# q and k of two batches loaded in 1 KB pieces, cast on chip and transposed by products with the identity

## The chip, the cores and the metric

The kernel runs on one core of a Trainium2 chip. The metric is device time in microseconds (us) of one execution, lower is better. The core has a matrix engine (PE, with its weight loads shown apart as PEld), a vector engine (DVE), a scalar engine (ACT), a general engine (POOL) and a synchronising engine (SP). PE writes only to PSUM, a memory of eight banks of 512 fp32 columns by 128 partitions, from which DVE or ACT must copy ("evacuate") results to SBUF. Transfers from and to DRAM (HBM) are DMAs: here they are issued from POOL's queue or from SP's queue and are carried by the same 16 DMA engines.

## The reference

Inputs are q, k, v of shape 8 x 8 x 576 x 64 (batch, head, position, head dimension) and three weights, all fp32. A sliding-window attention with a distance bias per head is followed, batch by batch, by a token-mixing layer:

```python
scores = scale * np.matmul(q, k.transpose(0, 1, 3, 2))
rel = pos[:, None] - pos[None, :]
mask = (rel >= 0) & (rel < window)                      # window = 128
scores = np.where(mask, scores + bias[None], -1000000000.0)   # bias = -slope[h] * |rel|
attn = softmax(scores)
x = (attn @ v) with the heads side by side              # 8 x 576 x 512
wq = x @ w_q;  wk = x @ w_k                             # 512 -> 64
W_tok = scale * np.einsum('bsd,btd->bst', wq, wk)
mixed = np.einsum('bst,btd->bsd', W_tok, x)
out = np.maximum(mixed, 0.0) @ w_out                    # 8 x 576 x 512, fp32
```

## The kernel before, in words

All products run in fp16 with fp32 sums in PSUM. The 576 positions of a batch are four blocks of 128 and a tail of 64; tails are handled for two batches at once. For every batch `b` the kernel does these steps, whose names are used below:

- **Loads.** Tiles `nat` hold a block of q or k (index `j` is 0 for q, 1 for k; `n` is the block): partition = position, columns = 8 heads of 64. Tiles `vt` hold blocks of v with a column of ones beside each head; `natt` and `vtl` hold the tails. For batches 1 to 7 POOL issues these loads, and the DMA itself turns fp32 into fp16 (L501, L508, L512, L516). For batch 0 alone, SP loads q and k as fp32 into tiles `natf` (function `lf`, L549), in runs of 64 values (256 B), and DVE or ACT casts them into `nat` (names `Cq0.n`, `Ck0.n`, at L365 and L367, the copy helper).
- **TQ, ETQ.** PE transposes `nat` (L361, in transpose mode, fp16 into PSUM; 16 small products a block) so that the head dimension lies on the partitions, and DVE or ACT evacuates into `qkT` (L371 and L373, two fp16 values moved as one fp32 on ACT). Batch 0 is done one block at a time, the others two at a time. TT and ETT do the same for the tails.
- **QK, EXP, MUL.** For each block `g` and half of the heads `u`, PE computes scores (QK), ACT applies the exponential (EXP, L674) and DVE multiplies with a table that holds the exponential of the bias and zero outside the window (MUL, L681). The result is `pt`. The tables `bias` and `biasl` are made at the start.
- **PV, X.** PE multiplies `pt` with v; the ones column gives the sum of the weights, and DVE divides (L723, L724) to give `x`.
- **XT, WQ, WK, G, MX, RM, OUT, EO, DO.** The mixing layer, reordered so that no 576 x 576 matrix is formed: x is transposed, multiplied with w_q and w_k, G is a 64 x 512 product of wk and x, MX multiplies wq with G, RM applies max(0, .) and writes fp16, OUT multiplies with w_out, EO copies to an fp32 tile `osb` (L365, L367) and DO stores it (L913, L916).

The order of the instructions on each engine is made by a planner inside the kernel (class `Order`). Each step has a list of the engines that may run it with a time for each, its dependencies, and a wish for its place (the table `WANT`, one number for each step). The planner repeatedly takes the engine that can start first, and among the steps that could start there within 0.11 us the one with the lowest number. Its result is a fixed order; on the chip the engines wait for each other through semaphores. While the planner's time is below 30 us, `keep_busy` (L392) puts products with the zero tile `fill` into PE's gaps, as many as the planner expects to fit; they write to the PSUM pair that the next step will use.

Three more things matter below. Each of the two DMA queues has eight semaphores, taken in turn, so an issue waits until the eighth transfer before it on that queue has landed. The outputs of batches 0, 1, 6 and 7 are stored by SP as soon as they are made; those of batches 2 to 5 (`LATE`) are kept in SBUF buffers (`HELD` = 18, shared with `natf`) and stored by POOL once all loads have been issued. POOL runs its set-up (identity, index and mask tables, clearing of padding) ahead of most loads. ACT's table of functions is loaded by its first instruction.

Of the kernel before, what the change touches and what calls it, by code (L numbers as in the profile page):

```python
# [33 lines left out]
STRIDE = 14  # L34
# [3 lines left out]
HELD = 18  # L38
LATE = (2, 3, 4, 5)
COLD = 8.0  # L40
# [4 lines left out]
    "ident": -516.89, "idh": -64.27, "iota": -947.82, "dist": -823.27, "zeros": -897.48,  # L45
# [153 lines left out]
}  # L199


# [802 lines left out]
```

## Time and profile before

| what | value |
|---|---|
| runs | 146.28, 146.66, 148.61 us, median 146.66 |
| profiled execution | 147.05 us, of which 145.3 us from its first to its last instruction (its span) |
| granted PE clock, mean over the span | 0.988 of full speed |
| busy in the span | PE 126.8, PEld 80.0, DVE 116.7, ACT 114.3, POOL 104.8 us |
| moved by DMA | 25.64 MB in 117447 packets, 113072 of them under 512 B |
| POOL's loads of q and k | 56, 128 KB each as written, median 6.4 us to landing |
| POOL's loads of v | 32, 128 KB each, median 6.6 us to landing |
| SP's loads of batch 0 | 8, 256 KB each, medians 4.5 (q) and 4.8 us (k) to landing |

Busy time is the union of an engine's instructions. Matmul ends are modelled, so PE's share is an upper bound for its use. "to landing" counts from the issue to the last byte's semaphore. Rows of the timeline name the line, the engine, the operation and the tiles, output first, then how many instructions were merged, and in brackets the idle time before them with what ended it.

### The profile page before, as it was taken

To read this page: it belongs to the slowest core of one execution; us is meant where nothing else is said; L and a number is where in the kernel's file an instruction comes from. 1 tells how busy PE (TensorE), PEld (TensorE's weight loads), DVE (VectorE), ACT (ScalarE), POOL (GpSimd) and SP (SyncE) were. 2 spreads that over 40 slices of the span, in tenths; PEclk is the share of its full clock that TensorE was granted. 3 is DMA by queue.
4 is the path that set the end of the run, shared out by engine and by line. 5 is a ranking of instruction groups with operands and counts; after the bars stand their busy time and mean duration, and the time that the engine had idled before them with its cause. 6 is when DMAs were issued, how large, how long until landed. Compare 5 with 4: busy or idle time off the path is not lost.

```text
span 145.3 us, 5428 instructions
## 1 busy us (share of the span) xinstructions
PE 126.8 (87%) x2315; PEld 80.0 (55%) x2315; DVE 116.7 (80%) x256; ACT 114.3 (79%) x169; POOL 104.8 (72%) x139
## 2 busy tenths in 40 slices
PE   6858858888997899779998997989999999999990
PEld 2224546645774458645674575647767657566340
DVE  6977997599839698959979999799999999991410
ACT  3727895599588976899599986999889989956751
POOL 5999678999986997578999999998977701230000
PEclk9986999999999999999999999999999999999999
DMA  4999999999999999999999999999999941155255
GB/s 103 262 182 180 159 154 144 149 173 154 190 251 186 157 183 218 247 179 155 156 155 156 157 154 157 154 154 151 146 213 399 363 171 72 77 144 207 83 162 202
DMA packets 117447, 25.64 MB, mean 177 GB/s; under 512 B 113072, under 2 KB 114096, under 8 KB 117424
## 3 DMA queue, kind: packets, MB, share of 16 engines
q0 software_dynamic: 106336, 18.49, 155.3%
q1 hardware_dynamic: 11088, 6.82, 16.6%
q8 instruction: 18, 0.29, 0.8%
q14 instruction: 5, 0.04, 0.1%
HBM read 29.62 MB, written 9.44 MB: 269 GB/s over the span
## 4 chain that ended last, share of the span: by engine, by line
PE 48%; DVE 16%; ACT 16%; POOL 7%; DMA 6%; issue 4%; POOLq 0%; DVEq 0%; ACTq 0%
PE pair L358 41%; ACT pt L674 10%; PE pair L361 7%; DMA vt<-in_v_dram 6%; DVE pt L681 3%; DVE x L724 3%; POOL nat L501 2%; DVE rm L837 2%; ACT qkT L371 2%; DVE xT L373 2%; DVE qkT L373 1%; POOL vt L516 1%; DVE inv L723 1%; POOL natt L508 1%; DVE xtl L724 1%
## 5 line engine op out<-in xcount | busy, mean ns | idle before, releaser
L674 ACT ACTIVATE pt<-pair 128x1024 f16<-128x1024 f32 x64 | 62.8, 1038 | 6.1 <-PE pair L358 5.8
L681 DVE TENSOR_TENSOR pt<-pt,bias 128x1024 f16<-128x1024 f16 x48 | 31.7, 683 | 3.3 <-ACT pt L674 3.1
L516 POOL DMA_DIRECT2D vt<-in_v_dram x32 | 29.7, 949 | 3.7 <-DMA nat<-in_k_dram 1.9
L358 PE MATMUL pair<-wout_sb,rm 128*128 128x512 f16 (+1 forms) x132 | 31.5, 373 | 0.7 <-ACT pt L674 0.5
L501 POOL DMA_DIRECT2D nat<-in_q_dram x28 | 25.9, 931 | 3.3 <-DMA vt<-in_v_dram 1.1
L501 POOL DMA_DIRECT2D nat<-in_k_dram x28 | 25.7, 925 | 1.6 <-DMA vt<-in_v_dram 0.5
L358 PE MATMUL pair<-qkT 64*128 64x256 f16 (+2 forms) x320 | 22.8, 254 | 4.0 <-ACT qkT L371 2.6
L358 PE MATMUL pair<-vt,pt 128*128 128x65 f16 x512 | 22.6, 193 | 1.4 <-DMA vt<-in_v_dram 1.0
L358 PEld LDWEIGHTS <-pt 128*128 128x128 f16 x576 | 20.0, 97 | 5.8 <-issue 2.5
L724 DVE TENSOR_TENSOR x<-pair,inv 128x512 f16<-128x512 f32 x32 | 22.1, 691 | 1.1
L365 ACT COPY osb<-pair 128x512 f32<-128x512 f32 (+1 forms) x25 | 14.8, 590 | 6.9 <-PE pair L358 6.7
L371 ACT COPY qkT<-pair 128x1024 f32<-128x1024 f32 (+2 forms) x19 | 16.0, 842 | 4.5 <-PE pair L361 3.5
L358 PEld LDWEIGHTS <-qkT 64*128 64x128 f16 x320 | 11.2, 95 | 12.4 <-issue 5.9
L358 PEld LDWEIGHTS <-rm 128*128 128x128 f16 x132 | 11.4, 97 | 12.0 <-issue 1.1
L913 POOL DMA_DIRECT2D out_dram<-osb x16 | 8.8, 558 | 11.0 <-DVE osb L367 5.4
L361 PEld LDWEIGHTS <-nat 64*128 64x128 f16 x512 | 9.4, 96 | 6.8 <-issue 4.6
L361 PE MATMUL pair<-identh,nat 64*128 64x64 f16 x512 | 11.2, 192 | 1.8 <-DVE x L724 0.4
L358 PE MATMUL pair<-fill 128*128 128x512 f16 x23 | 9.0, 531 | 3.1 <-DVE qkT L373 1.2
L358 PE MATMUL pair<-xT,wqq_sb 128*128 128x256 f16 (+1 forms) x64 | 10.3, 287 | 0.8 <-DVE xT L373 0.8
L681 DVE TENSOR_TENSOR pt<-pt,biasl 128x1024 f16<-128x1024 f16 x16 | 10.8, 683 | 0.2 <-ACT pt L674 0.2
L837 DVE TENSOR_SCALAR rm<-pair 128x512 f16<-128x512 f32 x16 | 10.5, 681 | 0.1
L367 DVE COPY osb<-pair 128x512 f32<-128x512 f32 (+1 forms) x12 | 8.0, 665 | 2.8 <-PE pair L358 2.7
(65 smaller groups left out, 162.7 us busy)
## 6 DMA issues: line engine op xcount, KB each, us to landing
vt<-in_v_dram POOLq DMA_DIRECT2D x32, 128.0 KB, 6.6
out_dram<-osb POOLq DMA_DIRECT2D x16, 256.0 KB, 4.6
out_dram<-osb SPq DMA_DIRECT2D x15, 256.0 KB, 5.4
nat<-in_k_dram POOLq DMA_DIRECT2D x28, 128.0 KB, 6.4
nat<-in_q_dram POOLq DMA_DIRECT2D x28, 128.0 KB, 6.4
natf<-in_q_dram SPq DMA_DIRECT2D x4, 256.0 KB, 4.5
natf<-in_k_dram SPq DMA_DIRECT2D x4, 256.0 KB, 4.8
out_dram<-osb SPq DMA_DIRECT2D x6, 128.0 KB, 2.4
```

Source lines behind the costliest of these rows:

```text
L358: hold(nc.tensor.matmul(*a, **k))
L361: hold(nc.tensor.transpose(*a))
L365: hold(nc.scalar.copy(out_ap, in_ap))
L367: hold(nc.vector.tensor_copy(out=out_ap, in_=in_ap))
L371: hold(nc.scalar.copy(out_ap.bitcast(FP32), in_ap.bitcast(FP32)))
L501: return lambda: nc.gpsimd.dma_start(out=nat_s[b % NNAT][j][n], in_=src[b, :, P * n:P * n + P, :].transpose([1, 0, 2]))
L516: return lambda: nc.gpsimd.dma_start(out=vt_s[b % NV][t][:, :, 0:D], in_=v[b, :, P * t:P * t + P, :].transpose([1, 0, 2]))
L674: nc.scalar.activation(out=pt[:, 0:1024], in_=two(s.bank).rearrange("p e c -> p (e c)"), func=AF.Exp, scale=SCALE)
L681: ENG2[o.eng].tensor_tensor(out=pt[:, 0:1024], in0=pt[:, 0:1024], in1=bt, op=ALU.mult)
L724: nc.vector.tensor_tensor(out=x[r].rearrange("p (g h d) -> p g h d", g=2, h=4), in0=pxv[r, :, :, 0:64], in1=inv[r].unsqueeze(3).broadcast_ ...
L837: hold(nc.vector.tensor_scalar(out=out_ap, in0=in_ap, scalar1=0.0, scalar2=WSCALE, op0=ALU.max, op1=ALU.mult))
L913: q.dma_start(out=out[b, P * st:P * st + P, c], in_=osb)
```

## The change

Batches 0 and 1 (`WIDE` = 2) now both take the way over `natf`. A tile is loaded by two DMAs, one for the even and one for the odd heads; on each partition lie four consecutive positions of one head, 1 KB in one piece. The cast regroups the blocks of 64 so that a pair of heads lies side by side. In place of 16 transposes a block, 16 ordinary products with a 64 x 64 identity write fp32 into every 4th column of two PSUM banks, so that the four positions come out interleaved in the right order. Each bank holds the heads of one unit `u` and is evacuated by itself; the scores of a unit need only its own halves. All loads from POOL wait for a tiny copy (`gate`) that reads the second q tile. Batch 1's outputs join the late ones, `HELD` is 23 and serves all full-width outputs, `keep_busy` puts in more fills, and all of `WANT` is different, so that the order of nearly every engine changes. By the instruction order, ACT's first instruction is now a cast, and the load of its function table stands behind that cast's wait for the second DMA; the load of `wq` moves from POOL's first to its twelfth; PE has 56 products with `fill` where it had 23.

```diff
-STRIDE = 14
+STRIDE = 14.6
-HELD = 18
-LATE = (2, 3, 4, 5)
-COLD = 8.0
+HELD = 23
+LATE = (1, 2, 3, 4, 5)
+COLD = 6.0
+GATE = (0, 1)
+WIDE = 2
...
-        n = int((gap + 0.3) / (0.43 if op.start < COLD else 0.216)) if gap > 0.1 else 0
+        n = int((gap + 0.5) / (0.43 if op.start < COLD else 0.216)) if gap > 0.1 else 0
...
-        issue = add(*name, want, {"POOL": (occ, occ + 1.5)}, deps, lambda o: emit())
+        issue = add(*name, want, {"POOL": (occ, occ + 1.5)}, [*deps, *gate], lambda o: emit())
...
         def lf(j, n):
             natf = spool.tile([P, DM], FP32, name="natf", tag="late", bufs=HELD)
-            src = (q, k)[j][0, :, P * n:P * n + P, :].transpose([1, 0, 2])
+            src = (q, k)[j][b, :, P * n:P * n + P, :].rearrange("(c e) (g r) d -> e c g (r d)", e=2, r=4)
 
             def em(o):
-                nc.sync.dma_start(out=natf.rearrange("p (h d) -> p h d", h=H), in_=src)
+                for e in range(2):
+                    nc.sync.dma_start(out=natf[:, 256 * e:256 * e + 256], in_=src[e])
 
             def cv(o):
-                cp(o.eng, nat_s[0][j][n].rearrange("p h d -> p (h d)"), natf)
-
-            d = add("L" + "qk"[j], 0, f"f{n}", next(i), {"SP": (0.92, 1.55)}, [], em)
-            d = od.add("Q", 0, n, 0.0, {"Q": (0.92, 1.7)}, [d], lambda o: None)
-            loads[0, j, n] = add("C" + "qk"[j], 0, n, next(i), EV(0.62, 0.43), [d], cv)
+                cp(o.eng, nat_s[b][j][n].rearrange("p (r e) d -> p e r d", e=2),
+                   natf.rearrange("p (e r d) -> p e r d", e=2, r=4))
+
+            d = add("L" + "qk"[j], b, f"f{n}", next(i), {"SP": (0.68, 1.3)}, first[-1:], em)
+            first.append(d)
+            d = od.add("Q", b, n, 0.0, {"Q": (0.66, 1.2)}, [d], lambda o: None)
+            if (b, j, n) == (0, *GATE):
+                gate.append(add("gate", "", "", -50, {"POOL": (0.1, 0.12)}, [d],
+                                lambda o: nc.gpsimd.tensor_copy(out=seen, in_=natf[:, 0:1])))
+            loads[b, j, n] = add("C" + "qk"[j], b, n, next(i), EV(0.62, 0.43), [d], cv)
...
+    def add_tq0(b, n, want):
+        def quad(o, h):
+            return one((o.bank[0], h)).rearrange("p (j c t) -> p j c t", j=2, c=2)
+
+        def em(o):
+            for j in range(2):
+                for i in range(4):
+                    for h in range(2):
+                        r = slice(64 * h, 64 * h + 64)
+                        mm(quad(o, h)[:, j].rearrange("p c (g i) -> p i c g", i=4)[:, i],
+                           nat_s[b][j][n][r, 2 * i:2 * i + 2, :].rearrange("p a b -> p (a b)"), identh[r, r],
+                           start=True, stop=True)
+
+        t = add("TQ", b, n, want, pe(0.47), [loads[b, 0, n], loads[b, 1, n], idh], em, banks=2, mode=1)
+        tq[b, n] = t
+        evt[b, n] = []
+        for h in range(2):
+            def ev(o, h=h):
+                cp(o.eng, qkT_s[b][:, :, 2 * h:2 * h + 2, P * n:P * n + P], quad(t, h))
+
+            evt[b, n].append(add("ETQ", b, f"{n}.{h}", want + 0.6, EV(0.60, 0.69), [t], ev, frees=[t], half=h))
...
-            evt[b, n] = ev
+            evt[b, n] = [ev, ev]
...
-        need = [evt[b, g], evt[b, g + 1]] if g < 3 else [evt[b, 3], ett[b]]
+        need = [evt[b, g][u], evt[b, g + 1][u] if g < 3 else ett[b]]
...
-            held = b in LATE
-            box["o"] = spool.tile([P, n], FP32, name=f"osb{n}", tag="late" if held else f"osb{n}",
-                                  bufs=HELD if held else 5 if n == DM else 2)
+            box["o"] = spool.tile([P, n], FP32, name=f"osb{n}", tag="late" if n == DM else f"osb{n}",
+                                  bufs=HELD if n == DM else 2)
...
-        for ns in ([0], [1], [2], [3]) if b == 0 else ([0, 1], [2, 3]):
+        for n in range(4) if b < WIDE else ():
+            add_tq0(b, n, base(b, 0) - 4 + 1.5 * n)
+        for ns in ([0, 1], [2, 3]) if b >= WIDE else ():
```

More of the change, by code (lines that the diff above doesn't have):

```diff
@@ L37 @@
 LAG = 0.5
-HELD = 18
-LATE = (2, 3, 4, 5)
-COLD = 8.0
-WANT = {
-    "ident": -516.89, "idh": -64.27, "iota": -947.82, "dist": -823.27, "zeros": -897.48,
[153 rows of a table removed]
+HELD = 23
[3 more added lines that the diff above has]
+WIDE = 2
+WANT = {
+    "ident": -513.47, "idh": -132.27, "iota": -510.12, "dist": -221.48, "zeros": -289.89,
[154 rows of a table added]
 }
@@ L313 @@
     ppool = ctx.enter_context(tc.tile_pool(name="psum", bufs=1, space=bass.MemoryType.PSUM))
+    seen = cpool.tile([P, 1], FP32, name="seen")
     fill = cpool.tile([P, 512], F16, name="fill")
@@ L530 @@
     wts = wto = None
-    late, issues = [], []
+    late, issues, gate, first = [], [], [], []
     loads = {}
@@ L578, in add_loads @@
             lv(0), lv(1), lt(), lv(2), lv(3), lvt()
+        elif b < WIDE:
+            for n in range(4):
+                lf(0, n), lf(1, n)
         else:
@@ L584, in add_loads @@
             wts[0] = add("wqq", "", "", -5, DVE(0.25), [wts[0]], mk_wqq)
-        if b:
+        if 0 < b < WIDE:
+            lv(0), lv(1), lt(), lv(2), lv(3), lvt()
+        elif b:
             lq(0, 2), lv(1), lq(1, 2), lq(0, 3), lv(2), lq(1, 3), lt(), lv(3), lvt()
```

307 rows, old and new, of the table WANT are left out of this document.

## The prediction

> **What bounds the kernel now.** First the page's busy shares: PE 87%, DVE 80%, ACT 79%, so three engines are near each other and none is the whole answer. Second the 40 slices (3.63 us each): PE shows gaps in the first eight or so and is near 9 afterwards, so the start is a stage of its own. Third the busy time by stretch (columns: stretch, its length, busy time of each engine, granted PE clock, DMA share, GB/s):
>
> ```profile
> 5.00:10.00 5.00, 2.69 (x37) 1.04 (x35) 4.76 (x12) 3.00 (x9) 5.00 (x8) 0.97 1.25 218
> 10.00:15.00 5.00, 4.25 (x53) 2.08 (x54) 3.54 (x6) 3.41 (x6) 4.78 (x6) 0.69 1.91 184
> 15.00:20.00 5.00, 3.80 (x84) 2.68 (x83) 4.76 (x11) 4.37 (x6) 3.15 (x4) 1.00 2.43 157
> ...
> 40.00:50.00 10.00, 8.82 (x183) 5.69 (x183) 6.30 (x13) 9.21 (x14) 7.87 (x10) 1.00 2.10 202
> ...
> 110.00:120.00 10.00, 9.62 (x215) 6.31 (x212) 9.77 (x21) 8.98 (x14) 4.40 (x9) 1.00 0.77 298
> ```
>
> In the first 30 us PE is busy 22.98 us by these rows, and 9.0 of that are products with the zero tile `fill`: 14.0 us of real work. From 30 us on it is busy 103.8 of 115.3. Fourth the chain of waits, which says why the start is thin:
>
> ```profile
> 7.50 2.04 POOL vt L516 x2
> 9.53 3.45 POOL nat L501 x4
> 12.99 8.91 DMA vt<-in_v_dram
> 21.90 0.04 issue
> 21.94 0.63 PE pair L358 x15
> ```
>
> The chain runs through POOL's load issues and a v tile that lands 8.9 us after issue. Fifth the timeline of ACT: where its exponentials (EXP, L674) stand.
>
> ```profile
> 10.74 1.94 ACT L674 ACTIVATE pt<-pair 128x1024 f16<-128x1024 f32 x2 [0.71 <-PE pair L358]
> ...
> 17.09 3.77 ACT L674 ACTIVATE pt<-pair 128x1024 f16<-128x1024 f32 x4 [0.49 <-PE pair L358]
> ...
> 23.86 1.96 ACT L674 ACTIVATE pt<-pair 128x1024 f16<-128x1024 f32 x2 [1.74 <-PE pair L358]
> ...
> 30.65 5.60 ACT L674 ACTIVATE pt<-pair 128x1024 f16<-128x1024 f32 x6
> ```
>
> Batch 0's eight end at 20.86, two of batch 1 at 25.8, and the other six wait until 30.65, because the second half of batch 1's q, k is transposed only at 28.46. So the start is bound by loads, what follows by PE with ACT and DVE close behind.
>
> **The change part by part.**
>
> *Loads on SP.* Eight loads of 1024 pieces of 256 B become 32 DMAs of 128 pieces of 1 KB. SP issued a 128-row output in 0.332 us (its median), so a 256 KB tile costs 0.66 us of issue, where the old ones took 0.43 to 1.61. The old tiles of batch 0 landed from 3.7 to 15.2 us (the cast of the last began at 15.19). Landing of a new piece: above 2.0 us (shortest output), below 3.0 (shortest old load, twice the bytes); I take 2.4. Eight may be in flight, so the ninth waits for the first, at about 3.1, when SP is there anyway. Batch 0 is then complete near 9 to 10 us, batch 1 near 17, with POOL's loads beside them.
>
> *Loads on POOL.* Eight of 104 go, 0.93 us each (L501 rows): its stream ends about 7 us before the old 105. Nothing waits for that end: outputs held for later follow it. The loads now wait for a copy that needs q tile 1's first piece: issue 2.07, landed 4.5. POOL's own set-up (0.68 of weight-load issue gone from its front, memsets moved ahead of the mask) ends near 4.6, so the wait costs about nothing; without that cover it would hold all v loads. First load near 5.0, before 5.73. The load of wq goes from first to twelfth; it lands near 24, and its two copies on DVE (0.6) precede WQ of batch 0, due near 25.5 and ahead of batch 1's scores in PE's order. Those wait for evacuations until about 26, which hides it; each us later than that is a us lost.
>
> *Casts.* 8 become 16: before 7 on DVE at a mean of 0.753 and one on ACT at 0.603; after, by the order of instructions, 12 and 4. The spread matters:
>
> ```profile
> L367 DVE CAST nat<-natf x7: 414/760/1459, 4.7 to 15.2; 128x512 f16<-128x512 f32 x7
> ```
>
> The long ones stand beside POOL's memsets, 0.56 to 0.86 beside its issues, 0.43 with POOL idle (15.19). The new cast also permutes blocks of 64. I take 0.56; ends 0.41 and 0.86.
>
> *Transposes and evacuations.* 128 transposes with fp16 output become 128 products with fp32 output in every 4th column. Sixteen transposes took 0.40 us (13.55). No row has the strided fp32 write: between 0.40 and twice that per tile, I take 0.40, the same array work; the other end adds 3.2 us of PE in all. What grows surely is the evacuation. Before: four of 1024 fp16 (0.685 on DVE, 0.586 on ACT) and two of 2048 (1.021): 4.6 us. After: 16 halves of 128x512 fp32, 10 on ACT at 0.60 and 6 on DVE at 0.69 (the output copies' rows): 10.1 us. Counting every form in both orders at the old durations, ACT goes from 114.3 to 119.4 and DVE from 116.7 to 121.8.
>
> The granted clock was 0.50 at 10 to 12 us and 0.73 at 12 to 14, and 0.92 or more elsewhere. The Trainium skill, "TensorE: Matmul & The Clock Gate", Part 4: PE-mode transpose, says that transposes do not count as activity for the clock gate as products do; by that rule the new products would keep the clock up, worth at most 1.4 us of the 3.9 busy there, and the sum would be 145.0 if PE were what is late then.
>
> *Set-up.* ACT's table load (1.28 us, at 0.73 before) now stands behind the wait for the second piece: 1.07 + 2.4 = 3.5. Then table to 4.8, q0's cast to 5.4, the bias exponentials (2.56) to 7.95; before they ended at 6.94. Queued behind: the first evacuation.
>
> *Filling products.* 23 become 56, in gaps the planner expected. Five stand ahead of the second transposed tile and five ahead of the first scores. A fill took 0.216 to 0.53; I take 0.3.
>
> *Outputs of batch 1* go from SP to POOL's late queue and all full outputs share 23 buffers: 23 held outputs in batches 1 to 5, so none waits. Nothing.
>
> **The sum, by a schedule of the start.** DVE, after the same memsets, casts k0 by 5.5; transposed tile 0 runs at 6.1 to 6.5 (11 fills end at 6.06 as before). Its halves leave at 8.0 (DVE) and 8.5 (ACT behind the bias). DVE then casts q1, builds a bias copy (0.6), casts k1: 9.8. Tile 1 to 10.5, halves out 11.1, five fills and scores: first EXP 12.1 (10.74 before). Two EXPs at a pitch of 0.94 to 14.0, two halves, two EXPs and a tail evacuation to 17.8; tile 3 waits for DVE's last cast, which stands behind two mask products, a normalisation and a tail copy: 18.1. Its half leaves ACT at 19.1, four EXPs end at 23.4 (20.86 before). Then batch 1 has its data: 10 halves and casts 5.1, eight EXPs 7.5, other copies 2.8 end at 38.8, masks at 39.4 (36.97 before). By then PE has done within 0.2 us the same real work as before at 36.97 (fewer output products, but the next x and q tiles). **Lag 2.4 us.**
>
> Given back: PE had 97.6 us of work left at 36.97 and 10.7 idle; 3.7 of it lay before 70 us, where batches ran with little ahead. In 70 to 130 it idles 2.6 in 60. At that rate idle is 1.3 from 39.4 to 70, 2.6, 0.5 to 139.5 and 3.8 at the end: 8.3. In the tail the first x transposes and WQ of the last batch now stand ahead of the last normalisations; before, their evacuation (0.6 of ACT at 131.85) held the chain: -0.4. Span 39.4 + 97.8 + 8.3 - 0.4 = 145.1, against 145.3. The profiled execution took 147.05, 1.75 more than its span; the median 146.66 is 1.36 more. **146.4 us**, no change.
>
> **Rivals.**
>
> *PE full from the start (faster).* If casts take 0.43 and fills 0.216, the schedule gains 1.4 by the checkpoint: lag 1.0; and if early data lets PE run as in 100 to 130 (idle 0.5 of 30) throughout, idle is 1.5 + 0.5 + 3.8. Span 38.0 + 97.6 + 5.8 - 0.4 = 141.0, time 142.4. For it: the gaps at 40 to 70; against: there ACT was busy 9.2 of 10, not waiting for loads.
>
> *Evacuations bind (slower).* ACT and DVE get 10.2 us more, all before 40 us, where both are full in my schedule. With casts at 0.86 and fills at 0.5 the lag is 4.2, and if nothing is given back the span is 41.2 + 97.8 + 10.7 - 0.4 = 149.3, time 150.7. It turns slower once lag less give-back passes 2.9. For it: DVE 89.8 and ACT 87.3 of 100 in 30 to 130; against: both idle 17 us in the first 30.
>
> *v starves (slower).* POOL loads issued from 7.5 took until after 15 while SP's stream ran. SP now moves 4 MB in all. If POOL gets nothing until 17.3, its fourth load, v tile 1, lands near 21.8; PE's order has its product ahead of batch 0's third scores, due 18.3: 3.5 more, 149.9. For it: v landed in 5.2 to 9.9. By the Trainium skill, "DMA: Bandwidth & Descriptors", Queues, rings and completion order, each engine alternates between the queues it has work for, packet by packet; by that rule POOL is slowed and not stopped, and this rival loses half its price.
>
> *The pieces land no sooner.* Then batch 0 still completes near 15 and only the costs remain: about 148, within 2%.
>
> **How the numbers follow.** 2% is 2.9 us, about what a measurement of this kernel can tell from no change. Forecast 0.38, pieces no sooner 0.05: same 0.43. PE full 0.32. Evacuations 0.17, v 0.08: slower 0.25. The forecast alone spans 144.0 to 149.0 by the casts, fills and products. The range takes in the rivals: 142.0 to 150.5.
>
> **What would show it.** Batch 0's last cast before 12 us in data, though later in DVE's order; first EXP 11.3 to 13; batch 0's eighth EXP 22 to 24.5; no ACT gap between 24 and 36; POOL's last load near 98; DVE near 121.8 and ACT near 119.4 busy; PE idle in 40 to 70 below 2 us. Wrong if first EXP comes before 10.5, if PE waits on v before 25, or if the strided products take over 0.6 a tile.

## The result, and the profile after

The changed kernel takes **182.86 us** (median, 182.75 to 183.9), the kernel before 146.77 beside it: **1.249 times** as long, 95% interval 1.242 to 1.255. The forecast was 146.4 with a range of 142.0 to 150.5. The profiled execution took 182.75 us, its span 180.7, so what lies around the span (2.05) is no explanation: the span grew by 35.4.

The stretches of the changed kernel that answer to those shown of the kernel before (stretch, length, busy time of PE, PEld, DVE, ACT, POOL, granted PE clock, DMA share, GB/s):

```profile
5.00:10.00 5.00, 1.02 (x11) 0.35 (x10) 0.49 (x2) 3.43 (x8) 0.00 (x0) 0.80 0.27 91
10.00:15.00 5.00, 3.44 (x21) 1.30 (x21) 2.51 (x6) 1.40 (x5) 4.05 (x6) 0.52 0.72 116
15.00:20.00 5.00, 2.97 (x25) 1.33 (x25) 1.12 (x2) 2.50 (x3) 3.26 (x4) 1.00 2.89 167
...
40.00:50.00 10.00, 2.51 (x21) 0.94 (x20) 2.23 (x4) 2.37 (x4) 2.05 (x3) 0.67 0.72 94
...
110.00:120.00 10.00, 9.66 (x180) 6.15 (x179) 9.62 (x20) 9.84 (x15) 8.77 (x12) 1.00 3.10 134
```

From 70 us on the changed kernel runs as the old one did (PE 9.6 of 10 at 110 to 120). Everything is lost before: at 40 to 50 us PE, DVE, ACT and POOL are idle about three quarters of the time or more and the DMAs move 94 GB/s, where they moved 202 before. Nobody computes too much; nothing arrives. The chain of waits says what does not arrive:

```profile
3.31 7.58 DMA natf<-in_q_dram
11.13 0.92 POOL natt L512
12.05 0.91 POOL vt L520
12.96 0.94 POOL natt L512
13.90 20.07 DMA vt<-in_v_dram
34.25 27.70 DMA wq_sb<-in_moe_w_q_dram
62.40 1.57 PE pair L362 x7
```

The step of the second q tile, which the gate on POOL's loads waits for, ends at 10.9 us; a v tile takes 20.1 us, the load of w_q 27.7. ACT's exponentials (L711) and the group of casts (busy us, mean ns, idle before it and its releasers) tell the same:

```profile
18.08 1.94 ACT L711 ACTIVATE pt<-pair 128x1024 f16<-128x1024 f32 x2 [0.93 <-PE pair L362]
...
39.23 1.94 ACT L711 ACTIVATE pt<-pair 128x1024 f16<-128x1024 f32 x2 [2.09 <-PE pair L362]
64.02 1.02 ACT L711 ACTIVATE pt<-pair 128x1024 f16<-128x1024 f32 x1 [6.26 <-PE pair L362]
```

```profile
L371 DVE CAST nat<-natf 128x512 f16<-128x512 f32 x12 | 5.5, 461 | 23.1 <-DMA natf<-in_k_dram 14.0 <-DMA natf<-in_q_dram 9.2
```

Batch 0's eight exponentials end at 41.2 us (20.9 before, 23.4 in the forecast), batch 1's begin at 64.0. The casts themselves are quick (0.46 us), but DVE stood idle 23.1 us for their tiles. The rows of SP's queue show the loads crawl (start, time for the two DMAs of a tile):

```profile
0.74 1.37 SPq L554 DMA_DIRECT2D natf<-in_q_dram  x2
...
8.03 3.16 SPq L554 DMA_DIRECT2D natf<-in_q_dram  x2
...
22.23 4.58 SPq L554 DMA_DIRECT2D natf<-in_q_dram  x2
...
53.16 4.35 SPq L554 DMA_DIRECT2D natf<-in_k_dram  x2
```

By the landings that the trace records, the first eight DMAs of 128 KB land 1.5 us apart (5.0, 6.5, 8.0 and so on, to 15.6 us); from then on, with POOL's loads beside them, mostly 2.1 to 2.4 us apart. From the sixth DMA on, SP's issue of a DMA ends only when the fifth before it has landed (within 0.7 us), so SP's rows show the same pace, 4.2 to 4.6 us a tile. (The kernel's semaphores alone would let eight be in flight; in same_order_16, below, it is eight. Why it is five here stays open.) Batch 0 is complete at 32.6 us and batch 1 at 68.3; the forecast had 9 to 10 and 17. POOL's loads landed about 4.25 us apart meanwhile (25.5, 29.7, 34.0, and later 43.2, 47.4, 51.7, 55.9).

### The profile page after: what moved, and what is told of

It is laid out like the page before. It is cut to its first block, busy times and chain, and to the rows that moved or that the text cites. A ratio compares the mean times of both kernels' runs of the same rounds, so it can differ in the third digit from the quotient of the medians.

```text
span 180.7 us, 5544 instructions
## 1 busy us (share of the span) xinstructions
PE 140.8 (78%) x2348; PEld 85.7 (47%) x2348; DVE 119.0 (66%) x265; ACT 119.1 (66%) x178; POOL 100.9 (56%) x138
## 4 chain that ended last, share of the span: by engine, by line
PE 46%; DMA 31%; DVE 15%; ACT 2%; issue 2%; POOL 2%; SPq 1%; DVEq 0%; ACTq 0%
PE pair L362 41%; DMA wq_sb<-in_moe_w_q_dram 15%; DMA vt<-in_v_dram 11%; PE pair L365 5%; DMA natf<-in_q_dram 4%; DVE pt L718 4%; DVE rm L874 3%; DVE x L761 2%; SPq L554 1%; DVE xT L377 1%; POOL natt L512 1%; DVE wqT L371 1%; DVE qkT L377 1%; ACT pt L711 1%; DVE osb L371 1%
## 5 line engine op out<-in xcount | busy, mean ns | idle before, releaser
L711 ACT ACTIVATE pt<-pair 128x1024 f16<-128x1024 f32 x64 | 63.4, 1035 | 14.4 <-PE pair L362 14.3
L362 PE MATMUL pair<-vt,pt 128*128 128x65 f16 x512 | 24.9, 198 | 9.5 <-DMA vt<-in_v_dram 8.7
L505 POOL DMA_DIRECT2D nat<-in_q_dram x24 | 21.6, 903 | 12.3 <-DMA vt<-in_v_dram 7.0
L505 POOL DMA_DIRECT2D nat<-in_k_dram x24 | 21.5, 901 | 7.3 <-DMA vtl<-in_v_dram 3.6
L362 PE MATMUL pair<-fill 128*128 128x512 f16 x56 | 20.3, 513 | 2.9 <-DVE fill L486 1.2
L371 DVE CAST nat<-natf 128x512 f16<-128x512 f32 x12 | 5.5, 461 | 23.1 <-DMA natf<-in_k_dram 14.0
L369 ACT CAST qkT<-pair 128x512 f16<-128x512 f32 x10 | 5.7, 583 | 18.8 <-PE pair L362 18.8
L760 DVE RECIPROCAL inv<-pair 128x8 f32<-128x8 f32 (+1 forms) x40 | 8.1, 203 | 12.8 <-PE pair L362 12.5
L362 PEld LDWEIGHTS <-rm 128*128 128x128 f16 x132 | 11.1, 97 | 11.3 <-issue 1.1
L362 PE MATMUL pair<-identh,nat 64*128 64x64 f16 x128 | 6.9, 268 | 11.2 <-DVE nat L371 8.0
L362 PE MATMUL pair<-xT,wqq_sb 128*128 128x256 f16 (+1 forms) x64 | 10.9, 296 | 5.9 <-DVE wqq_sb L466 5.7
L949 POOL DMA_DIRECT2D out_dram<-osb x20 | 10.9, 548 | 2.7 <-DMA out_dram<-osb 0.7
L872 ACT ACTIVATE rm<-pair 128x512 f16<-128x512 f32 x21 | 11.8, 604 | 0.3 <-ACT pt L711 0.2
L375 ACT COPY qkT<-pair 128x1024 f32<-128x1024 f32 (+1 forms) x10 | 9.5, 954 | 3.5 <-DVE qkT L377 1.6
```

Source lines behind the costliest of these rows:

```text
L362: hold(nc.tensor.matmul(*a, **k))
L369: hold(nc.scalar.copy(out_ap, in_ap))
L371: hold(nc.vector.tensor_copy(out=out_ap, in_=in_ap))
L375: hold(nc.scalar.copy(out_ap.bitcast(FP32), in_ap.bitcast(FP32)))
L505: return lambda: nc.gpsimd.dma_start(out=nat_s[b % NNAT][j][n], in_=src[b, :, P * n:P * n + P, :].transpose([1, 0, 2]))
L711: nc.scalar.activation(out=pt[:, 0:1024], in_=two(s.bank).rearrange("p e c -> p (e c)"), func=AF.Exp, scale=SCALE)
```

## Experiments: what the loads are carried by

Each experiment has a short name, given in brackets where it comes up. The theory, A: a DMA is dealt out over the DMA engines along its outermost dimension. The new load (`e c g (r d)`, one `e` at a time) has the four head pairs `c` there, so four engines carry it; the old one had 128 positions. The rival, B: 1 KB pieces, SP's queue or the new work are slow by themselves. In the expectations quoted here "57.9" stands for the end of SP's stream in the changed kernel; that is about when its last issue ends (57.5), and its last tile lands at 68.3.

**The same four DMAs a tile with outermost dimension 32 and 2** (four_outer32 and four_outer2)**.** Both load each tile in four DMAs, one 64 KB quarter each, and differ in the outermost dimension; every engine's instructions otherwise stay.

```diff
-                for e in range(2):
-                    nc.sync.dma_start(out=natf[:, 256 * e:256 * e + 256], in_=src[e])
+                for c in range(4):      # outermost 32; the other kernel puts e (2) outermost
+                    nc.sync.dma_start(out=natf[32 * c:32 * c + 32].rearrange("g (e x) -> g e x", e=2),
+                                      in_=src[:, c].rearrange("e g x -> g e x"))
```

> The changed kernel with its own layout, each tile loaded by four DMAs of 64 KB, one for each head pair, whose outermost dimension is 32. Same pieces, twice as many DMAs. Theory A: 64 issues at 0.55 us end near 35 us and that is when the last tile of batch 1 lands; the time is 150 to 158 us. Theory B: eight of half the size in flight, so the stream takes about 58 us or longer and the time is 183 or more.

> The changed kernel, each tile loaded by four DMAs of 64 KB whose outermost dimension is 2; number and size of the DMAs are those of the run with four DMAs of outermost dimension 32. Theory A: two engines carry each, a 64 KB DMA takes about 2 us as a 128 KB one on four did, the stream ends near 58 x 2 = 116 us and the time is near 240 us. Theory B: the same as that other run.

Measured: 160.76 us with 32, 248.25 with 2 (one execution of each timed). Same bytes, same pieces, same queue, same number of DMAs; 87 us apart. Theory A holds, B falls. (With 32 the time is 3 over what A expected. SP's issues are short, 0.43 us in the median. The DMAs land 0.47 us apart until 9.2 us; then POOL's loads come beside them, the landings slow down, and the last lands at 48.9 us and not near 35.) The packet records of the traces show the number directly. Time for which so many of the 1 KB packets of SP's loads were under way at once, in us:

```
                 1      2      3      4     5 and more
outermost 2    29.4   97.3    3.4    0.1    0
outermost 4     1.6    9.1    8.9   42.2    3.8     (the changed kernel)
outermost 32    1.8    1.6    1.0    1.2   21.3     (same_order_16, below; mostly 6 to 15)
```

The records of the semaphores fit: a load leaves 3 updates with outermost 2, 5 with 4 and 16 with 32. In the changed kernel one of the five comes right behind the issue (1.9 us for the first DMA) and four when data has landed (4.6 to 5.0).

The Trainium skill, "DMA: Bandwidth & Descriptors", section "Why a DMA increments its semaphore by 16 and not by 1", states it: the number of engines is the largest one up to 16 that divides the slowest dimension (other than 1) of both access patterns. These traces agree for 2, 4 and 32 (packets and updates above).

**Outermost dimension 32 in two DMAs** (outer32, then same_order_16)**.** The first kernel puts (group, head pair) on the partitions, so that a PSUM bank holds half of the positions of all heads instead of all positions of half the heads, and a unit's scores need both halves. The planner knows that dependency, and its order of PE, DVE and ACT is another one.

```diff
-            src = (q, k)[j][b, :, P * n:P * n + P, :].rearrange("(c e) (g r) d -> e c g (r d)", e=2, r=4)
+            src = (q, k)[j][b, :, P * n:P * n + P, :].rearrange("(c e) (g r) d -> e g c (r d)", e=2, r=4)
...
-        need = [evt[b, g][u], evt[b, g + 1][u] if g < 3 else ett[b]]
+        need = [*evt[b, g], *(evt[b, g + 1] if g < 3 else [ett[b]])]
```

> The changed kernel with one thing turned round: on the partitions of a loaded tile the head pair now runs fastest and the group of four positions slowest, so that the DMA's outermost dimension is 32 where it was 4; the two halves of a transposed block then hold positions instead of head pairs. Pieces (1 KB), DMAs (32 of 128 KB), bytes and the eight in flight stay. Theory A (a DMA is dealt out by its outermost dimension, so that each ran on 4 of the 16 DMA engines): the stream of q, k on SP ends near 18 us, where issue at 0.55 us each ends, instead of 57.9; POOL's loads land 6 to 9 us after issue; the time is that of my schedule, 145 to 149 us. Theory B (1 KB pieces, or eight DMAs in flight on this queue, are slow in themselves): the stream still ends near 58 us and the time stays near 183.

Measured 168.51 us (1.150, interval 1.143 to 1.158): between both expectations, with SP's last tile at 29.7 us but gaps on PE all through the run. The loads and the order had changed at once. The next kernel (same_order_16) has the same loads and keeps the order: each product picks its heads from all 128 partitions through a strided view of the identity, banks and dependencies stay as in the changed kernel, and so does the order of every engine, instruction for instruction.

```diff
...
-                           nat_s[b][j][n][r, 2 * i:2 * i + 2, :].rearrange("p a b -> p (a b)"), identh[r, r],
+                           nat_s[b][j][n][:, 2 * i:2 * i + 2, :].rearrange("p a b -> p (a b)"),
+                           identh.rearrange("p (g c) -> p c g", c=4)[:, 2 * h:2 * h + 2, :],
...
```

> The changed kernel with one thing altered: the partitions of a tile hold (group, head pair) instead of (head pair, group), so that the outermost dimension of each load is 32 and not 4, and each product with the identity picks its 64 of the 128 partitions through a strided view of the identity. Every engine's instruction order is the same as in the changed kernel, instruction for instruction. Theory A (a load is carried by as many DMA engines as its outermost dimension allows, and nothing else is badly wrong): SP's stream ends near 30 us instead of 57.9, as in the first variant with outer dimension 32, POOL's early loads land within 7 us each, and the time falls to 144 to 153. Rival C (SP's and POOL's streams collide even on 16 engines, and that made the first variant 168.5): 164 to 170 here too. Rival D (the new instruction order is itself worse than the old one, even with early data): 154 to 163, with PE gaps after 70 us that the changed kernel does not show.

Measured **152.07 us**, 1.031 (1.022 to 1.040). Its stretches:

```profile
5.00:10.00 5.00, 3.05 (x22) 1.53 (x21) 2.99 (x8) 4.08 (x11) 4.02 (x6) 0.95 1.05 187
10.00:15.00 5.00, 4.56 (x32) 2.86 (x31) 2.07 (x5) 1.21 (x2) 5.00 (x7) 0.71 1.81 214
...
40.00:50.00 10.00, 9.65 (x205) 6.61 (x203) 9.43 (x19) 9.21 (x14) 9.65 (x12) 1.00 3.09 154
```

With the same order, 30.8 of the 36.1 us go with the outermost dimension, although the products with the identity are slower here (1.12 us a tile, 0.62 in the changed kernel). The exponentials from the ninth on come 30.4 to 32.2 us earlier here than in the changed kernel, and the last one 30.4 (162.7 and 132.4). So the changed kernel has lost all of this by the start of its second batch, and rivals C and D fall; the time lies in theory A's window. The 16.4 us between this kernel and the one before it go with the other order that the planner made there (two_both, below, has the products and loads of that kernel in this order and takes 153.9). SP's rows in this kernel:

```profile
0.74 1.33 SPq L554 DMA_DIRECT2D natf<-in_q_dram  x2
...
11.17 1.25 SPq L554 DMA_DIRECT2D natf<-in_q_dram  x2
...
23.18 1.44 SPq L554 DMA_DIRECT2D natf<-in_k_dram  x2
```

A tile now costs SP 1.25 us of issue, 0.62 a DMA; the forecast took 0.33 from the stores. Batch 0 lands at 17.2, batch 1 at 30.0. The issue is only part of that: batch 0's sixteenth DMA is issued by 11.1 us, and it lands 6.6 us after its start, with POOL's loads beside it, where the first took 2.6.

**Is it w_q?** (after_wq_first) The changed kernel's longest step of the chain is the load of w_q, moved from first to twelfth of POOL's.

```diff
+    dma_w(wq_sb, moe_w_q)()          # ahead of POOL's set-up, in place of its twelfth load
```

> The changed kernel with one thing altered: the load of w_q is POOL's first instruction behind its constants, as in the kernel before, and no longer its twelfth load; every other instruction keeps its place. In the changed kernel the copies of w_q wait for it until 62.0 us and batch 1's scores stand behind the product that needs them. Theory A (the loads on four engines bind, w_q is one of several that they make late): batch 1's last tiles land near 57.9 all the same; 177 to 183. Rival Q (the late w_q is itself the cause): below 170.

Measured 182.51 us (1.240, 1.229 to 1.252): no change. The step that ended the longest wait of the chain was a consequence: behind it batch 1's own tiles were as late.

**An earlier gate** (gate_first)**.** POOL's loads wait for the first q tile instead of the second (`GATE = (0, 0)`).

> The changed kernel, but POOL's loads wait for the first q tile instead of the second. The copy then waits until about 6.6 us instead of 10.95. If POOL's late start is what costs: 4 us less, near 179. If the loads are held up afterwards by the SP stream on the same engines (theory A): the stream still ends near 58 us, and the time is within 2 us of 183.

Measured 203.8 us (one timed execution). Neither expectation is met, and it settles little: the planner knows the gate, and with another gate it made another order. What it does show: POOL's first eight loads land 5.5 to 6.4 us earlier (16.1 to 45.9 us), and SP's last tile 5.3 us later (73.5). SP's landings, 1.5 us apart in the changed kernel until 15.6 us, are mostly 2.1 to 2.3 apart here from 7.7 us on. So each queue slows the other.

## Experiments: the five microseconds that are left

same_order_16 is still 5.2 us over the kernel before. Its span can be put against the old one's by real PE work (all products less those with `fill`). By 40 us the old kernel had done 22.9 us of it (31.84 busy, 8.95 with `fill`), this one 17.5 (34.68 and 17.17): a lag of 5.4. The work in all is 119.8 against 117.8: +1.9, the products with the identity, 1.12 us a tile here. From 40 to 130 us PE idles 3.6 against 6.0: -2.4. Behind 130: +0.15. Together 5.0, which is the difference of the spans (150.3 and 145.3). So the question is the lag.

**The other way round: the kernel before with only batch 0's loads in 1 KB pieces** (before_1k_batch0; one DMA a tile, `g c e (r d)`, eight products of 128 columns, one evacuation of 1024 fp32), its order kept.

> The kernel before, its order kept, with only batch 0's q and k moved to the new way: one 256 KB load a tile in 1 KB pieces (outer dimension 32), a cast that regroups, eight products of 128 columns a tile with the identity into every 4th fp32 column, and one evacuation of 1024 fp32 columns instead of 1024 fp16. Theory A: the tiles land earlier than before (last one below 12 us instead of 15.2), but the start then waits for POOL's v loads and for four evacuations that are 0.35 us longer each; 144 to 148, within 2%. Rival E (early q and k of batch 0 is what the start lacks): the first 37 us shrink by 3 or more, 141 to 143.5. Rival F (1 KB pieces on 16 engines take their bandwidth from POOL's loads, so v is later): 149 to 152.

Measured 150.69 us, 1.022 (1.013 to 1.030). Batch 0 is complete at 10.95 us instead of 15.2, as forecast, and it does not help: the first four tiles land no sooner (3.8, 4.9, 6.6, 7.3; before 3.7, 5.4, 6.3, 7.2). ACT's timeline has the first exponentials at

```profile
12.28 1.94 ACT L685 ACTIVATE pt<-pair 128x1024 f16<-128x1024 f32 x2 [0.49 <-PE pair L358]
```

against 10.74, behind products of 1.1 us and evacuations of 1.0 and 1.2. The price is that of rival F, but not its mechanism: POOL's eighth load lands at 16.7, before at 19.8.

**One change at a time on same_order_16**, each with the order of every engine kept: one DMA a tile; then products of 64 partitions again (bank = half of the positions, scores wait for both halves); then an exponential of one zero column at the front of ACT's queue, so that the table loads early. They are one_dma_16, halves_16 and halves_16_table, each on top of the one before.

```diff
-                for e in range(2):
-                    nc.sync.dma_start(out=natf[:, 256 * e:256 * e + 256], in_=src[e])
+                nc.sync.dma_start(out=natf.rearrange("p (e x) -> p e x", e=2), in_=src)
...
+    nc.scalar.activation(out=early, in_=fill[:, 0:1], func=AF.Exp)
```

> Against the variant with outer dimension 32 and the changed kernel's order (152.07 us): one thing more, each tile of q or k is loaded by one DMA of 256 KB instead of two of 128 KB. Theory S (SP's issue, 0.62 us a DMA whatever its size, is what holds the loads once all engines carry them): batch 0 lands by 11 to 12 us instead of 17.2, batch 1 by 18 to 21 instead of 30.0. If late data is what the 5.2 us over the kernel before are, the time falls to 146 to 149. Theory L (in that variant the start waits for the chain of first evacuations and products, not for data: batch 0's last cast ran at 20.6, 3.4 us after its data had landed): 151 to 152.5, and the eighth exponential of batch 0 stays within 1 us of 27.7.

> Against the one-DMA variant: the products with the identity take 64 of the 128 partitions again, as in the changed kernel (16 products of 64 rows and 64 columns; a bank now holds half of the positions of all heads, so that scores wait for both halves; each engine's order is unchanged). Products fall from 1.12 us a tile (1.9 at half clock) to 0.62 (1.04 at half clock). If the first chain binds the start (L), the eighth exponential comes 1 to 3 us earlier and the time is 1.5 to 3 below the one-DMA variant; if data binds (S), no change beyond 0.7.

> Against the halves variant: one instruction is added, an exponential of one zero column at the front of ACT's queue, so that ACT loads its table near 1.2 us instead of behind the wait for the first loaded tile (4.25 us). If the first chain binds (L): the bias exponentials end 1.3 earlier, the first score exponential comes at 12 to 13 (14.4 in the outer-32 variant), and the time falls by 0.7 to 1.5 more, to 147 to 149; if S, nothing.

Measured 154.82 us (1.056, 1.051 to 1.061), 155.36 (1.056, 1.048 to 1.064) and 154.72 (1.054, 1.049 to 1.059). All expectations of a gain are missed: the first is 2.7 slower than with two DMAs, the other two change nothing. Yet the single steps did what they were meant to. SP's issue is 0.61 us whether a DMA has 128 or 256 KB, batch 0 lands at 10.6 and batch 1 at 20.7 in the last of them, almost as forecast, and its first exponential starts at 10.85. What PE then waits for, in its timeline:

```profile
17.17 0.41 PE L363 MATMUL pair<-vt,pt 128*128 128x65 f16 x8 [2.69 <-DMA vt<-in_v_dram]
...
20.92 0.60 PE L366 MATMUL pair<-identh,natt 64*128 64x64 f16 x15 [2.62 <-DMA natt<-in_k_dram]
21.45 3.48 PE L363 MATMUL pair<-fill 128*128 128x512 f16 x8
```

This is what the forecast's rival of starving v describes: POOL's first load lands at 14.9 (10.5 in same_order_16), its fourth at 22.3 (the rival had 21.8), and batch 0's eighth exponential ends at 30.9. And eight filling products, meant for a gap of the plan, stand behind the wait and take 3.5 us at a granted clock of 0.54 (21 to 25 us).

**Slower on SP, no fills, no gate.** On halves_16_table, batch 1's tiles go back to two DMAs (paced); then the 45 fills behind the first eleven are left out (paced_no_fill); then the gate's copy (paced_no_fill_no_gate).

> Against the variant with one DMA a tile, half-partition products and the early table load (154.72 us): batch 1's tiles go back to two DMAs of 128 KB each, batch 0's stay at one of 256 KB. Theory V (with one DMA a tile SP issues 4 MB in 12 us and POOL's loads starve: in that variant PE waited 2.7 us for a v tile until 17.2, 2.6 us for the tail of k until 20.9, and eight filling products behind that took 3.5 us at a low clock): SP's slower issue of batch 1 lets POOL's loads through, these waits shrink below 1 us each, and the time falls to 147 to 150. Rival W (batch 0's 2 MB alone already starve them): 152 to 155.

> Against paced: the 45 filling products behind the first eleven are left out (they compute nothing that is used). Theory F (they were placed in gaps of a planned time that data does not keep, so they run late, in front of real work): 1 to 4 us faster. Rival G (they keep the granted clock up, which is worth as much): within 1 us, with a granted clock near 0.5 to 0.7 in more of the first 30 us.

> Against paced_no_fill: the copy that POOL waits for ahead of its loads is left out, so POOL's first load goes out at about 4.4 instead of 6.2 us; the orders are the same otherwise. If the gate delays v (V): 0.5 to 1.8 faster. If the engines are simply shared, SP's first tiles land later by what POOL's land earlier: between 0.5 faster and 1 slower. The forecast had the gate at nothing.

Measured 151.51 us (1.030, 1.025 to 1.034), 151.38 (1.030, 1.022 to 1.037), 151.69 (1.029, 1.021 to 1.037). Pace gives 3.2 us, but 151.5 lies between the windows of V and W, and neither is met; the waits for v and the tail fall to 1.13 and 0.84 in paced:

```profile
15.66 0.41 PE L363 MATMUL pair<-vt,pt 128*128 128x65 f16 x8 [1.13 <-DMA vt<-in_v_dram]
...
17.48 0.40 PE L366 MATMUL pair<-identh,natt 64*128 64x64 f16 x15 [0.84 <-DMA natt<-in_k_dram]
```

Fills and gate give nothing measurable. Without fills the granted clock is 0.50 at 10 to 20 us where it was 1.00, as rival G had it (the same two stretches, of paced first and of paced_no_fill second):

```profile
10.00:15.00 5.00, 3.63 (x35) 1.59 (x34) 2.71 (x6) 3.01 (x4) 4.73 (x6) 1.00 1.75 207
15.00:20.00 5.00, 3.50 (x54) 2.02 (x55) 2.54 (x6) 2.32 (x3) 1.44 (x2) 1.00 1.69 223
```

```profile
10.00:15.00 5.00, 2.02 (x24) 1.29 (x24) 2.83 (x5) 3.01 (x4) 4.63 (x6) 0.50 1.75 202
15.00:20.00 5.00, 2.95 (x48) 2.19 (x48) 2.42 (x6) 2.32 (x3) 1.44 (x2) 0.50 1.70 214
```

**Other splits, and the piece size itself.** Tiles loaded as before the change (pieces_256, on halves_16_table: one DMA, 1024 pieces of 256 B); two DMAs a tile for both batches (two_both, on paced); four for batch 1 (four_batch1, on paced).

```diff
-            src = (q, k)[j][b, :, P * n:P * n + P, :].rearrange("(c e) (g r) d -> g c e (r d)", e=2, r=4)
+            src = (q, k)[j][b, :, P * n:P * n + P, :].transpose([1, 0, 2])      # pieces_256
```

> Against the variant with one 1 KB-piece DMA a tile, half-partition products and the early table load (154.72 us): the tiles of both batches are loaded as the kernel before does it, 1024 pieces of 256 B a tile in one DMA (position on the partition), and the products read them accordingly; every order stays. Theory P (1 KB pieces are what makes SP's stream short, and a short stream helps): batch 0 lands after 15 us and batch 1 after 30, and the time is 156 to 162. Theory V (what the start lacks is POOL's v, which SP's stream delays; with 256 B pieces the two queues share the engines more evenly): v lands earlier than in that variant and the time is 150 to 154, so that the piece size by itself is worth nothing here.

> Against paced (151.51 us): batch 0's tiles too are loaded by two DMAs of 128 KB, so SP's issue (1.25 us a tile) paces both batches. Theory V: POOL's loads land earlier, PE's waits on v (1.3 us) and on the tail of k (0.8) go, and the time is 149 to 151. Rival S (batch 0's q and k, complete at 17 instead of 11 us, are then what is late): 151.5 to 153.

> Against paced: batch 1's tiles are loaded by four DMAs of 64 KB each (batch 0's stay at one), so SP's stream is slower behind batch 0. Theory V: POOL's eighth load lands before 24 us (25.9 in paced), and the time is 149.5 to 151. Rival S (batch 1's data comes too late, after 32 us instead of 24.8): 152 to 156.

Measured 155.41 us (1.061, 1.050 to 1.072), 153.92 (1.051, 1.042 to 1.059) and 153.53 (1.045, 1.032 to 1.057). 256 B pieces against 1 KB pieces, at the same number of DMAs and in the same order: 155.41 and 154.72, no difference that was measured, though SP's stream ends at 40.4 us instead of 20.7. The time lies between the windows of P (156 to 162) and V (150 to 154), so neither is met. POOL's first four loads land 1.4 to 3.1 us earlier, as V asked, and batch 1's tiles up to 20 us later; that the two cancel is likely, but was not tested. The two other splits go the way of S, two_both 0.9 beyond its window: each seems to trade one lateness for another. In two_both it is w_q that DVE, and behind it PE, wait for (DVE's timeline):

```profile
29.96 0.36 DVE L467 COPY wqq_sb<-wq_sb 128x256 f16<-128x256 f16 x2 [2.04 <-DMA wq_sb<-in_moe_w_q_dram]
```

In four_batch1 POOL's eighth load lands at 23.4 us as V asked, batch 0's eighth exponential ends at 23.9, near the forecast's 23.4, and batch 1's tiles then come at up to 39.0.

**Half of SP's stream taken away** (paced_half)**.** On paced, batch 1's loads are left out and its casts read batch 0's tiles, so batch 1's result is another one; all other work stays.

```diff
+            natf = kept.get((j, n)) or spool.tile([P, DM], FP32, name="natf", tag="late", bufs=HELD)
+            kept[j, n] = natf
...
-                else:
-                    for e in range(2):
-                        nc.sync.dma_start(out=natf[:, 256 * e:256 * e + 256], in_=src[e])
```

> Against paced (151.51 us): SP's loads of batch 1 are left out; batch 1's casts read batch 0's tiles, so batch 1's result is not the reference's, and all other work stays. Theory V (the two streams together cannot feed the first two batches in time; what one gains the other loses): POOL's eighth load lands before 22 us instead of 25.9, no engine waits long for a load, and the time falls to 146 to 149. Rival O (the new order and its work at the start, evacuations and casts, hold it, not loads): 150 to 152.

Measured 147.88 us (1.009, 1.004 to 1.014): V's window, and O falls. POOL's eighth load lands at 19.9 instead of 25.9, PE waits 0.2 us at most for a load, and 3.6 of paced's 4.3 us are gone. Its stretch from 10 to 15, against paced's above (PE 3.63, POOL 4.73 busy there), and the next:

```profile
10.00:15.00 5.00, 4.10 (x49) 2.17 (x49) 3.09 (x7) 3.02 (x5) 5.00 (x7) 1.00 3.48 136
15.00:20.00 5.00, 4.76 (x79) 3.04 (x75) 4.37 (x10) 2.97 (x5) 4.35 (x6) 1.00 3.47 132
```

So most of what paced still loses is supply too: in none of the splits tried do SP's and POOL's streams together bring what two batches need soon enough. No variant here beats the kernel before. That holds for paced_half too, although it reads 27.5 MB from HBM where the kernel before reads 29.6, and has batch 1's data with batch 0's: in this order even so much better a supply wins nothing over the kernel before. What stays open is where the rest of 0.4% to 1.4% in paced_half comes from, and why two DMAs a tile are worth 152.1 us with the slow products (same_order_16) and 153.9 with the quick ones and the early table (two_both); the late w_q accounts for the wait shown, but no run moved it there alone.

## Why the prediction was wrong

**The step that failed** is *Loads on SP*: "Landing of a new piece: above 2.0 us (shortest output), below 3.0 (shortest old load, twice the bytes); I take 2.4", and from it "Batch 0 is then complete near 9 to 10 us, batch 1 near 17". Both bounds came from rows whose outermost dimension is 128 partitions. The new access pattern, quoted in the change itself, has 4 there. The shape of the transfer was never compared with that of the rows it was priced by. Measured: the first DMA landed 4.3 us after its issue, at 5.0 us; the next ones followed 1.5 us apart, and 2.1 to 2.4 beside POOL's loads, where the forecast had issues 0.33 apart; the batches were complete at 32.6 and 68.3 us. 30.8 of the 36.1 us are this step (same_order_16). "Eight may be in flight" did not hold there either: it was five.

**The rival that should have been there.** "The pieces land no sooner" was priced at about 148, with batch 0 complete near 15 as before. There was no rival in which the pieces land later: that every load has all the engines was taken for granted.

**SP's issue**: 0.66 us a tile was taken from stores; measured 1.25 for two DMAs on 16 engines (0.61 to 0.62 a DMA, of 128 or 256 KB). With engines right this puts the last issue of batch 0 at 11.1 us; that the batch lands at 17.2 and not at 9 to 10 is as much the landing, 6.6 us for the last DMA beside POOL's loads and not 2.4.

**v starves**: named, priced at 3.5 us, given 0.08. The runs show the mechanism as soon as SP is fast (waits of 2.7 and 2.6 us in halves_16_table; pace gives 3.2 us back; half of SP's stream away gives 3.6 more, though it also gives batch 1 its data early). The supply of the two queues together is most of what the change costs on 16 engines. On the rule of arbitration packet by packet, which halved this rival: a POOL load is 1024 pieces, 64 an engine if it is spread over all 16; an SP load is 128 pieces on four engines, 32 each. If those four take equal numbers of pieces from both queues in turn, one POOL load lets two SP loads pass, 2 x 2.1 = 4.2 us; its landings in the changed kernel are 4.25 apart. In four_outer2 an SP load again has 32 pieces an engine, on two engines, and POOL's loads land 4.25 apart again (33.0, 37.2, 41.5, 45.7, 50.0). By that rule (the Trainium skill, "DMA: Bandwidth & Descriptors", "Queues, rings and completion order") the trace agrees, in so far as the turns are equal; how many pieces one turn takes, no run here shows. The error was to think that turns protect a queue that needs every engine from one that fills four.

**Lag and give-back.** With 16 engines the lag at 40 us is 5.4, not 2.4; the first exponential comes at 14.4 (forecast 12.1), the eighth ends at 27.7 (23.4). Given back: from 40 to 130 us PE idles 2.4 less, all of it between 40 and 70 (1.0 instead of 3.4), as the forecast had it. That step was right; the tail's -0.4 was +0.15.

**Terms.** Products: 0.62 us a tile at full clock and 1.06 at half (paced), not 0.40; by the forecast's own bound (0.6) this term is wrong. The 0.40 was a row of 16 transposes of a tail, of the same shape but with fp16 output; the range that the forecast gave, up to twice 0.40, holds. Casts 0.46 on DVE (0.56 taken), evacuations 0.58 and 0.69 (0.60 and 0.69), ACT busy 119.1 (119.4), fills 0.31 in same_order_16 (0.3): right. DVE 119.0, not 121.8, as the casts were quicker. POOL's last load goes out by 106 us even on 16 engines (98 in the forecast; before 105): eight loads fewer (of 106, not 104), but it starts later and waits for landings at 16 to 31 us. The gate costs nothing once engines are right (151.38 and 151.69), as forecast; on four engines it held POOL to 11.1 us. w_q: forecast to land near 24 and be hidden, it landed at 62.0; on its own it cost nothing there (after_wq_first).

**The clock rule** stays open. At 10 to 15 us the granted clock is 0.69 before with transposes and 0.71 in same_order_16 with products, but the two differ in what PE does then. In before_1k_batch0, where the order is kept and only batch 0's transposes became products, it is 1.00 in that stretch, as the rule has it, and the kernel is no faster. In paced_no_fill products alone did not keep it up (0.50); there the fills did (paced).

**What would have shown it**: first exponential by 13, eighth by 24.5, no ACT gap at 24 to 36. All three failed in the changed kernel (18.1, 41.2, gaps of 1.6 us and more), so the list did its work; the chances did not, with 0.25 on slower and nothing beyond 150.7.

## What to carry to other kernels

Before a rewritten load is priced by an old row, compare their access patterns, not their bytes: with a 4 in the outermost place loads of 128 KB landed 1.5 us apart alone and 2.1 beside another queue, where loads of 256 KB on 16 engines landed about 1.0 apart (before_1k_batch0), and the same data in another partition order made the kernel 30 us faster. When two queues feed one start, speeding one up can hold the other back, as it did here (POOL's first load at 14.9 us instead of 10.5): ask what the whole stage must receive by when. And where a planner makes the order, test a change of data with the order held fixed; here one added dependency, and the other order that came of it, went with some 15 us.

## What was not expected of the hardware

- SP's issue of a load on 16 engines takes 0.60 to 0.61 us in the median for 128 or 256 KB in 1 KB pieces; the 128-row stores take 0.33.
- Pieces of 256 B and of 1 KB gave the same time of the kernel (155.41 and 154.72 us) at the same number of DMAs.
- A queue whose loads have 1024 pieces each is slowed to the pace of a few engines when another queue keeps those few busy: POOL's loads landed 4.25 us apart beside 60 GB/s of SP traffic on four engines, and 4.25 us apart beside half of that on two (four_outer2).
- With four engines SP had five loads of 128 KB in flight, with 16 engines eight (the changed kernel and same_order_16).
